# One PSUM tile per bank, an exp per bank, a new recording order and filler products in a scheduled attention-and-convolution kernel

## Chip, cores, metric

The kernel runs on one core of one Trainium2 chip. The metric is device time in microseconds (us) of that core. A run over 1.5% above the fastest of its kernel is counted as slow. The medians below are of all runs, the ratios and their intervals of fast runs alone. The engines are called by their names in the profile: PE (TensorE matmuls), PEld (its weight loads), DVE (VectorE), ACT (ScalarE), POOL (GpSimd) and SP (SyncE, which only starts transfers here).

## The reference

Four batches, eight heads, 768 positions, 64 columns per head. Attention with 8 global keys and a window of 96, whose result `x` (4 x 768 x 512) goes into a gated long convolution. All inputs and outputs are float32.

```python
scores = (q @ k.T) / sqrt(64) + bias                  # bias: -slope[h] * distance
scores = where(is_global | is_local, scores, -1e9)
a = exp(scores - max);  a = a / (a.sum() + 1e-9)
x = (a @ v).transpose(0, 2, 1, 3).reshape(4, 768, 512)
x1, x2, x3 = split(x @ w_proj)                        # 512 columns each
conv = irfft(rfft(x2, axis=1) * rfft(filter), n=768)  # circular convolution over positions
out = (x1 * conv * x3) @ w_out
```

## The kernel before

The kernel first notes down every piece of work as an `Op`: with the engine or engines that may do it, an assumed cost, its inputs and outputs, and the PSUM bank that it fills (`acq`) or reads (`use`). A list scheduler (`Plan.schedule`) then decides engine, bank and order by these costs, and `emit` records the real instructions in the order of the scheduled starts. Waits between engines are not written by hand. The tile layer puts them in from what each recorded instruction reads and writes, by declared tile.

PSUM is declared as four tiles of two banks each. A `Bank` of the plan is one half of such a tile, or a whole one for the scores of two heads:

```python
self.psum = [self.ps.tile([P, 1024], F32, name=f"bank{i}") for i in range(4)]
...
def emit(self, order):
    for o in order:
        a = o.acq
        if a:
            lo = 512 * (a.at % 2)
            a.tile = self.psum[a.at // 2][:, lo:lo + 512 * a.n]
        o.fn(o.eng)
```

The choice of a bank prefers one whose sibling in the same tile is in use, so that pairs stay whole for the scores:

```python
if o.acq.n == 1:
    i = min(range(8), key=lambda i: (max(banks[i], at), banks[i ^ 1] == math.inf
                                      and -1 or 0, -banks[i]))
else:
    i = min((0, 2, 4, 6), key=lambda i: max(banks[i], banks[i + 1]))
```

Scores of a pair of heads fill two banks, and one exp of 864 columns reads both:

```python
def scores(self, hp, gi):
    b = g.bank(2)
    ...                                  # run: products of both heads, one bank per head
    g.op("P", 0.3, run, acq=b, ...)
    g.op("A", act(864), lambda _: nc.scalar.activation(eo, b.f32()..., Act.Exp,
         scale=self.scale), use=[b], w=[("E", hp, gi)], table="exp", name="exp")
    g.op("V", dve(864, 2) + ..., masked, ...)    # times the mask
```

Per batch, PE does: transposes of q and k, scores, values, transposes of the result, the gate's products (x1 and x3), the projection for x2, forward transform, inverse transform, output projection. Between any two of these, ACT or DVE empties banks into SBUF. While one batch is in its convolution, the next is in its attention.

The softmax here doesn't subtract the row's maximum and nothing guards it: scores larger than these inputs give would overflow.

## Time and profile before

| | before |
|---|---|
| time, median of 3 runs given with the kernel | 233.29 us (232.41 to 234.41) |
| time, median of 4 runs, with the profiled one | 232.85 us |
| span in the profile | 232.7 us |
| mean granted clock of PE | 0.947 of full speed |

From the page of the profile, busy time by engine, and then two rows of the span in 40 slices of 5.8 us: PE's busy share in tenths, and PE's granted clock in tenths.

```profile
PE 190.6 (82%) x1630; PEld 111.4 (48%) x1630; DVE 157.6 (68%) x381; ACT 145.1 (62%) x252; POOL 75.0 (32%) x96
...
PE   5473889798996797899989998999979889991871
...
PEclk9997667999999599999999999999999999999799
```

PE is the busiest engine by far, but its row is full of 7s and 8s even in the middle: it stalls often and briefly. The clock row has dips (5, 6, 7), where the throttle granted half speed for a while. The Trainium skill, "TensorE: Matmul & The Clock Gate", Part 1, says that the clock halves after an idle window of about 3.4 us. The trace agrees in the length: its slow stretches last 3.41 or 6.83 us. Before PE's last product there are four: at 20.4 (6.8 us), 30.7 (6.8), 75.0 (6.8) and 215.0 us (3.4). The trace has no record of the clock before 17.0 us, and the row shows 9s there.

The windows view by stage. The borders are the first gate products of batches 0, 1, 2 and 3, the last gate product and the end. Columns: stretch, its length, busy us and count of PE, PEld, DVE, ACT and POOL, granted clock, the transfer engines' share of busy time summed as that view does it, GB/s. (The borders were set 0.2 us ahead of the gate products: the timeline has the first at 36.30 us.)

```profile
36.10:94.30 58.20, 48.60 (x467) 29.90 (x466) 43.05 (x100) 36.20 (x66) 41.06 (x47) 0.93 1.98 121
94.30:129.40 35.10, 32.84 (x274) 18.45 (x275) 23.63 (x61) 22.36 (x40) 5.55 (x7) 1.00 0.60 77
129.40:173.30 43.90, 40.48 (x372) 23.87 (x372) 32.21 (x78) 31.90 (x58) 0.00 (x0) 1.00 0.10 37
173.30:195.60 22.30, 20.17 (x178) 12.03 (x178) 19.70 (x42) 11.47 (x22) 0.00 (x0) 1.00 0.02 8
195.60:232.70 37.10, 24.75 (x110) 10.80 (x107) 11.08 (x21) 16.15 (x32) 0.00 (x0) 0.95 0.21 82
```

PE bounds every stretch, with a few us missing in each; 36 to 94 us is the worst of the middle stages (48.60 of 58.20 us), and in the tail nothing else is left to fill PE (24.75 of 37.10).

From the starts of PE's instructions I split its time into streaming at full clock (what the columns need: 0.216 us per 512), what was lost to a halved clock, and stall. Before: 160.2 + 11.2 + 57.0 us, and the rest is the time before PE's first product. Stall between 40 and 200 us: 32.4 us. The half clock includes the start, where the clock is not recorded. Pages and traces do not give these sums; they are mine.

Where PE's stalls come from is half hidden: they look like ordinary waits for ACT and DVE, and ACT in turn waits for PE. The waits of ACT, by what it was to write and whom it waited for (us in total, times, longest):

```profile
ACT x L310 <- PE bank L682: 14.4, 17, 2.7
ACT eo L306 <- PE bank L746: 10.5, 11, 5.7
...
ACT ot L310 <- PE bank L769: 6.8, 8, 1.1
```

To tell proper waits from others, I matched each wait in the *built* program with its operands: does the wait ask for the instruction that wrote (or last read) this bank, or for a later one? I call the second kind late. Here is one, in the last output projection: the ACT evacuation of the first half of a tile needs PE's instruction no. 3219, but its wait asks for no. 3227, four products later (weight loads are numbered too), into the *other half* of that tile. In the trace that product ended 0.863 us later. The timeline of the tail shows what this looks like. First PE (start, duration, what, in brackets the idle time before and its releaser), then ACT:

```profile
215.02 5.39 PE L746 MATMUL bank<-inv,X 128*128 128x384 f16 x22 [3.65 <-DVE X L806]
221.41 0.59 PE L769 MATMUL bank<-wo,y 128*128 128x512 f16 x2 [1.00 <-ACT eo L306]
222.94 4.92 PE L769 MATMUL bank<-wo,y 128*128 128x512 f16 x22 [0.94 <-DVE y L758]
```

```profile
224.78 1.08 ACT L310 ACTIVATE ot<-bank 128x512 f32<-128x512 f32 x2 [3.42 <-issue]
226.23 1.09 ACT L310 ACTIVATE ot<-bank 128x512 f32<-128x512 f32 x2 [0.36 <-ACT ot L310]
227.95 1.09 ACT L310 ACTIVATE ot<-bank 128x512 f32<-128x512 f32 x2 [0.64 <-ACT ot L310]
```

The output stage begins at 221.41, but the first bank is emptied 3.4 us later, and from then on always two at a time (x2): both halves of a tile come free together.

Last, two groups from the page that the change touches: the exps (shape, count, busy us, mean ns, idle before), and the inverse transform, of which part runs at half clock.

```profile
L588 ACT ACTIVATE E<-bank 128x864 f16<-128x864 f32 x48 | 40.1, 903 | 1.6 <-PE bank L578 1.4
...
L746 PE MATMUL bank<-inv,X 128*128 128x384 f16 x96 | 20.9, 364 | 5.4 <-DVE X L806 3.7
```

### The profile page before, as it was taken

How to read it: one execution, taken by the hardware profiler on the slowest of the kernel's cores; microseconds unless marked ns; L12 is line 12 of the kernel's file. 1: busy time of each engine (PE TensorE's matmuls, PEld its weight loads, DVE VectorE, ACT ScalarE, POOL GpSimd, SP SyncE). 2: the span in 40 equal slices, each digit the busy share in tenths (PEclk: the TensorE clock that was granted, in tenths of full speed). 3: DMA queues.
4: the chain of work that ended last, by engine and by line, in shares of the span. 5: the costliest groups of instructions: out<-in, count | busy, mean ns of one | idle time of the engine just before them, and what ended most of it. 6: DMA issues, size and time to landing. Idle time of an engine off the chain costs nothing. (4 is left out here: it accounts for less than half of the span.)

```text
span 232.7 us, 4288 instructions
## 1 busy us (share of the span) xinstructions
PE 190.6 (82%) x1630; PEld 111.4 (48%) x1630; DVE 157.6 (68%) x381; ACT 145.1 (62%) x252; POOL 75.0 (32%) x96
## 2 busy tenths in 40 slices
PE   5473889798996797899989998999979889991871
PEld 2271656554444565555445656436545545340430
DVE  6894886764789777792188998617888796037230
ACT  4589882436897862524896848569974644662532
POOL 8999638987828636910000000000000000000000
PEclk9997667999999599999999999999999999999799
DMA  7999999999999979992400000150000001500015
GB/s 134 195 156 169 202 191 155 152 145 165 147 110 69 119 51 109 119 114 74 180 3 0 3 1 3 45 202 27 0 0 3 0 3 55 216 0 0 0 46 230
DMA packets 90933, 20.90 MB, mean 90 GB/s; under 512 B 83776, under 2 KB 87840, under 8 KB 90912
## 3 DMA queue, kind: packets, MB, share of 16 engines
q0 software_dynamic: 80912, 12.52, 78.3%
q1 hardware_dynamic: 10000, 8.10, 11.2%
q8 instruction: 13, 0.21, 0.4%
q14 instruction: 8, 0.07, 0.1%
HBM read 26.61 MB, written 6.29 MB: 141 GB/s over the span
## 5 line engine op out<-in xcount | busy, mean ns | idle before, releaser
L682 PE MATMUL bank<-xT,w 128*128 128x384 f16 x256 | 44.3, 329 | 2.6 <-ACT xT L306 1.4
L588 ACT ACTIVATE E<-bank 128x864 f16<-128x864 f32 x48 | 40.1, 903 | 1.6 <-PE bank L578 1.4
L682 PEld LDWEIGHTS <-w 128*128 128x128 f16 x256 | 25.1, 99 | 19.9 <-issue 3.6
L310 ACT ACTIVATE x<-bank 128x384 f16<-128x384 f32 x31 | 15.2, 491 | 25.0 <-PE bank L682 14.4
L600 DVE TENSOR_TENSOR E<-E,mask 128x864 f16<-128x864 f16 x32 | 18.4, 602 | 17.8 <-ACT E L588 17.7
L690 DVE TENSOR_TENSOR g<-bank,x 128x384 f16<-128x384 f32 x32 | 17.8, 557 | 14.2 <-PE bank L682 5.8
L322 POOL DMA_DIRECT2D kn<-in_k_dram x28 | 25.4, 920 | 5.5 <-DMA g<-in_moe_filter_fft_dram 2.9
L322 POOL DMA_DIRECT2D vn<-in_v_dram x28 | 25.0, 914 | 2.3 <-PE bank L625 1.4
L746 PE MATMUL bank<-inv,X 128*128 128x384 f16 x96 | 20.9, 364 | 5.4 <-DVE X L806 3.7
L769 PE MATMUL bank<-wo,y 128*128 128x512 f16 x96 | 22.5, 379 | 2.4 <-ACT eo L306 1.0
L578 PE MATMUL bank<-QT,KT 64*128 64x216 f16 (+2 forms) x224 | 17.1, 263 | 8.0 <-ACT E L588 3.2
L640 DVE TENSOR_TENSOR xn<-bank,rc 128x256 f16<-128x256 f32 (+1 forms) x48 | 22.5, 469 | 1.6
L310 ACT ACTIVATE ot<-bank 128x512 f32<-128x512 f32 x24 | 13.4, 595 | 14.3 <-PE bank L769 6.8
L306 ACT CAST eo<-bank 128x384 f16<-128x384 f32 x29 | 12.8, 488 | 14.0 <-PE bank L746 10.5
L322 POOL DMA_DIRECT2D qn<-in_q_dram x18 | 15.9, 891 | 16.0 <-PE bank L552 8.9
L620 PE MATMUL bank<-vn,E 128*128 128x65 f16 x224 | 18.8, 201 | 2.3 <-DVE xn L640 0.7
L539 PE MATMUL bank<-ab,fwd 128*128 128x512 f16 x72 | 18.3, 379 | 1.3 <-ACT ab L306 0.7
L620 PEld LDWEIGHTS <-E 128*128 128x128 f16 x224 | 16.1, 102 | 6.3 <-DVE E L600 2.9
L625 PE MATMUL bank<-vn,E 128*128 128x65 f16 x192 | 18.5, 200 | 0.0
L306 ACT CAST ab<-bank 128x512 f16<-128x512 f32 x24 | 13.8, 596 | 6.1 <-PE bank L726 4.6
L578 PEld LDWEIGHTS <-KT 64*128 64x128 f16 x224 | 9.3, 99 | 16.3 <-issue 12.8
L746 PEld LDWEIGHTS <-X 128*128 128x128 f16 x96 | 9.8, 109 | 13.2 <-issue 4.9
(100 smaller groups left out, 317.9 us busy)
## 6 DMA issues: line engine op xcount, KB each, us to landing
out_dram<-ot SPq DMA_DIRECT2D x24, 256.0 KB
kn<-in_k_dram POOLq DMA_DIRECT2D x24, 128.0 KB, 5.9
vn<-in_v_dram POOLq DMA_DIRECT2D x24, 128.0 KB, 6.4
qn<-in_q_dram POOLq DMA_DIRECT2D x18, 128.0 KB, 7.2
ot<-in_q_dram SPq DMA_DIRECT2D x6, 256.0 KB
w<-in_moe_w_proj_dram POOLq DMA_DIRECT2D x4, 256.0 KB, 7.0
g<-in_moe_filter_fft_dram POOLq DMA_DIRECT2D x1, 768.0 KB, 13.3
w<-in_moe_w_proj_dram POOLq DMA_DIRECT2D x1, 512.0 KB, 10.3
```

The lines of the kernel that those rows point to most:

```text
L306: {"A": nc.scalar.copy, "V": nc.vector.tensor_copy, "G": nc.gpsimd.tensor_copy}[e](out, in_)
L310: self.nc.scalar.mul(out, in_, c)
L322: return self.g.op(eng, {"G": 0.93, "S": 0.5}[eng], lambda _: e.dma_start(dst, src), w=w, r=r, nbytes=nbytes, name=name, bias=-2000.0 + se ...
L578: nc.tensor.matmul(sp[:, hh, off:off + w], self.KT[hs, hp, P * m:P * m + P], self.QT[hs, hp, KL * m:KL * m + w], start=(off == 0), stop=Tr ...
L588: g.op("A", act(864), lambda _: nc.scalar.activation(eo, b.f32().rearrange("p (h c) -> p h c", h=2)[:, :, 0:432].rearrange("p h (m w) -> p ...
L600: nc.vector.tensor_mul(eo, eo, mk[:, :, 0:2] if gi == 0 else mk[:, :, 1:3])
L620: nc.tensor.matmul(o[:, hh, i], ef[:, at:at + P], vt[:, t, 2 * hp + hh, :], start=first, stop=(t == 0), skip_group_check=True)
L625: nc.tensor.matmul(o[:, hh, i], ef[:, at:at + P], vt[:, t - 1, 2 * hp + hh, :], start=False, stop=True, skip_group_check=True)
L640: nc.vector.tensor_mul(xn[:, ts[0]:ts[0] + nt].rearrange("p t h d -> p h t d"), o[:, :, :, 0:D], r.to_broadcast([P, 2, nt, D]))
L682: nc.tensor.matmul(bk.f32()[:, 0:h], self.w[:, c, o + P * j:o + P * j + P], self.xT[:, c, h * s:h * s + h], start=(c == 0), stop=(c == 3))
L746: nc.tensor.matmul(bk.f32()[:, 0:h], X[:, s, cs], self.inv[:, s, :], start=(s == slots[0]), stop=(s == slots[-1]))
L769: nc.tensor.matmul(bk.f32(), y[:, c, P * t:P * t + P], self.wo[:, c, :], start=(c == 0), stop=(c == 3))
```

## The change

Its parts are: (1) eight tiles of one bank; (2) scores into two separate banks and an exp of 432 columns on each; (3) instructions recorded so that a consumer comes as soon as its producers are recorded, not by scheduled start; (4) products of zeros (`busy`) wherever the scheduler foresees that PE idles; (5), not in the change's own title, new cost figures in the scheduler, a free choice of bank, and the 768-column angle group of the tables split in two so that each fits a bank. The core of the diff:

```diff
-LAT = {"P": 0.22, "A": 0.16, "V": 0.14, "G": 0.12, "S": 0.1}
+LAT = {"P": 0.2, "A": 0.15, "V": 0.12, "G": 0.15, "S": 0.1}
+BEGIN = 1.0
@@ schedule: choice of banks, cost of transfers @@
-                    if o.acq.n == 1:
-                        i = min(range(8), key=... banks[i ^ 1] == math.inf and -1 or 0 ...)
-                    else:
-                        i = min((0, 2, 4, 6), key=lambda i: max(banks[i], banks[i + 1]))
+                    where = sorted(range(8), key=lambda i: banks[i])[:len(o.acq)]
-                dma[0] = max(dma[0], o.start + 1.7) + o.bytes / 300e3
+                dma[0] = max(dma[0], o.end + 1.8) + n * size / (306e3 if size < 512 else 390e3)
-        return out
+        return self.program(self.fill(out))
@@ new @@
+    BUSY = 0.225
+    def fill(self, out):
+        ...
+                gap = o.start - at                      # PE idle in the plan
+                n = int((gap - 0.1) / self.BUSY)
+                if n > 0:
+                    spare = [...]                       # a bank that nobody holds meanwhile
+                    if spare: ...                       # n products of `idle` (zeros) into it
+    def program(out):
+        ...                                             # need[o]: producers, and who held its bank
+        while len(order) < len(out):
+            for e in "AVSGP":                           # PE last
+                if line[e] and need[line[e][-1]] <= done:
+                    o = line[e].pop(); done.add(o); order.append(o)
+                    break
@@ buffers, scores, emit @@
-        self.psum = [self.ps.tile([P, 1024], F32, name=f"bank{i}") for i in range(4)]
+        self.psum = [self.ps.tile([P, 512], F32, name=f"bank{i}") for i in range(8)]
+    def busy(self, n, b):
+        for _ in range(n):
+            self.nc.tensor.matmul(b.f32(), self.idle[:, 0:P], self.idle, start=True, stop=True)
-        b = g.bank(2)
+        bs = [g.bank(), g.bank()]
-        g.op("A", act(864), lambda _: nc.scalar.activation(eo, b.f32()..., Act.Exp, ...), use=[b], ...)
+        for hh in range(2):
+            g.op("A", act(432), lambda _, hh=hh: nc.scalar.activation(
+                eo[:, hh], bs[hh].f32()[:, 0:432]..., Act.Exp, ...), use=[bs[hh]],
+                w=[("E", hp, gi, hh)], ...)
-                a.tile = self.psum[a.at // 2][:, lo:lo + 512 * a.n]
+                b.tile = self.psum[b.at]
```

Left out: the same edit of `acq=b` to `acq=[b]` everywhere, and further cost figures (scores 0.30 to 0.34, values 0.03 per product, transposes of the result 0.06, bank release +0.1).

## The prediction

> **What bounds the kernel now.** The page: PE busy 190.6 of 232.7 us (82%), DVE 68%, ACT 62%. From 36 to 205 us PE is the busiest engine in nearly every 10 us stretch (windows view). Before that data and ACT set the pace: ACT runs without a break from 15.3 to 25.7 us (timeline: masks, first exps), PE only 18.6 us of the first 30. After 205 us nothing overlaps; PE idles about 11 us. Comparing PE's starts in the trace with what the columns need at full clock, I estimate 160 us streaming, 12 us lost to a halved clock (granted clock 0.5 at 20-27, 31-37, 75-82, 215-218 us), 56 us of stalls, 33 of them between 30 and 205 us.
>
> **What the change removes.** I matched the waits of both built programs with their operands. Before, 125 of 169 waits of ACT for PE ask for a later product than the one that wrote the bank being read; so do 36 of 72 of DVE for PE and 94 of 283 of PE for ACT or DVE. After: 0, 0 and 2. In the trace the late part costs ACT about 30 us and PE directly 12.7 us, nearly all where PE is the bound. Zero products: 58; 15 in the start, 13 in the middle, 20 ahead of the last inverse (where PE waits 4.0 us for DVE), 10 ahead of the last output. A 512-column product takes 0.216 us at full clock, so the middle ones cost at most 2.8 us and the 20 fill that gap. The Trainium skill, "TensorE: Matmul & The Clock Gate", Part 1, says an idle window of 3.4 us halves the clock; the trace agrees (slow stretches are 3.41 or 6.83 us long).
>
> **What it adds.** 48 exps of 864 columns become 96 of 432. Back to back, five of 864 took 3.98 us (0.80 each), three of 384 took 1.27 (0.42); estimate 0.46 each, 5 us more ACT in all, 1.5 at the start where ACT is critical.
>
> **On the critical path.** Start to 36 us: up to 1 us lost, 1 to 2 gained by clock. Middle: of 12.7 direct about 10, about 4 from consumers that come sooner, about 4 from the stall at 73-77 us and the half clock after it, less 3 for zero products and exps. Tail: inverse at full clock 1.7 us (22 products at 0.32 now, 0.164 after), evacuations no longer held back in pairs 2 to 3: 4.5. Sum about 20.
>
> **Predicted: 213 us**, 206 to 221 in 8 of 10; faster by over 2% 0.94, within 2% 0.05, slower 0.01.
>
> **What would show it.** ACT idle before x, ot and eo with PE as releaser falls from 32 us to under 12. PE stall between 40 and 200 us roughly halves. Granted clock is 1.0 from 75 us on. The stretch from the last gate product to the end (36.7 us) shrinks to about 32. Up to 36 us nothing moves by over 2 us.
>
> **What would make it wrong.** DVE becomes the limit in the middle, so removed waits return as waits for DVE; loads of the second batch (DMA share over 90% to 85 us) come too late for a faster PE; zero products delay PE where the gap does not exist; the order from new cost figures is worse.

## More of the kernel before

Count of late waits in the built program before:

```
engine that waits <- engine waited for     late / all
ACT <- PE                                    78 / 169
DVE <- PE                                    36 /  72
PE  <- ACT or DVE                            94 / 283
```

For ACT the prediction has 125. That count took the 47 waits of exps for late as well, but one exp of 864 columns reads both halves of its tile, so it needs the later product. A second count, from the kernels built again, gives 78; it confirms the row of DVE, and for PE gives 92 of 281.

## The result, and the profile after

| | before | after |
|---|---|---|
| median of 4 runs | 232.85 us | 207.76 us (206.38 to 208.45) |
| ratio | | 0.8904, 95% interval 0.884 to 0.8969 |
| span in the profile, granted clock | 232.7 us, 0.947 | 204.3 us, 0.982 |

Ratios here are the mean time of one kernel's fast runs over that of the other's fast runs of the same rounds, so not quite the ratio of the medians beside them. The predicted 213 us was 5 us too high; the range held the result.

The page of the kernel after: busy times, PE's row, PE's clock row, and the chain that ended last by engine.

```profile
PE 191.8 (94%) x1688; PEld 111.9 (55%) x1688; DVE 152.2 (75%) x382; ACT 149.4 (73%) x303; POOL 75.5 (37%) x96
...
PE   7993799999998899999999999999999999999992
...
PEclk9998599999999999999999999999999999999999
...
PE 82%; ACT 11%; DVE 4%; issue 2%; ACTq 0%
```

PE's row is 9 almost throughout. Note that busy PE alone does not prove useful work, as 58 of the products are zeros; the sum below takes them out. The chain now runs along PE for 82% of the span. (Before, the chain could be followed for only 3% of the span, so there is nothing to compare.) The windows by the same stages:

```profile
33.00:76.90 43.90, 41.93 (x428) 26.41 (x425) 38.61 (x94) 34.24 (x73) 37.64 (x44) 1.00 2.53 157
76.90:111.00 34.10, 34.06 (x320) 20.05 (x320) 26.07 (x69) 24.89 (x51) 9.97 (x12) 1.00 1.10 106
111.00:151.20 40.20, 40.20 (x391) 24.16 (x388) 32.88 (x80) 32.56 (x71) 0.00 (x0) 1.00 0.13 42
151.20:171.40 20.20, 20.20 (x185) 12.41 (x184) 18.96 (x41) 12.65 (x29) 0.00 (x0) 1.00 0.04 15
171.40:204.30 32.90, 28.82 (x140) 13.36 (x138) 11.06 (x21) 17.39 (x31) 0.00 (x0) 0.99 0.23 88
```

From 76.9 to 171.4 us PE is busy 94.46 of 94.5 us: the records leave no idle time of PE there, so little is left to gain except by less work. The start (up to the first gate) went from 36.1 to 33.0 us, the middle from 159.5 to 138.4, the tail from 37.1 to 32.9. The first stretch of the middle alone gave 14.3 of the 28.4 us. (The profiled run of after is its fastest, 206.38 us; by the medians the gain is 25.1.) The loads that it runs under, which I had feared would be late, came at 157 instead of 121 GB/s.

The sum over PE, in us:

```
                streaming   half clock   stall   zero products   stall 40-200 us
before            160.2        11.2       57.0        0             32.4
after             160.2         6.6       22.6       12.5           12.0
```

The timeline of the tail after, first PE, then ACT:

```profile
185.63 3.19 PE L356 MATMUL bank<-idle 128*128 128x512 f16 x14
188.66 4.32 PE L803 MATMUL bank<-inv,X 128*128 128x384 f16 x24
192.81 2.32 PE L356 MATMUL bank<-idle 128*128 128x512 f16 x10
194.97 5.34 PE L826 MATMUL bank<-wo,y 128*128 128x512 f16 x24
```

```profile
196.09 0.60 ACT L364 ACTIVATE ot<-bank 128x512 f32<-128x512 f32 x1 [2.54 <-PE bank L826]
196.95 0.60 ACT L364 ACTIVATE ot<-bank 128x512 f32<-128x512 f32 x1 [0.27 <-PE bank L826]
```

The first output bank is emptied 1.1 us after its first product started (3.4 before), and then one by one, every 0.86 us, right behind PE's four products. In the built program no wait of ACT or DVE for PE is late any more (0 of 263, 0 of 125), and 2 of 417 of PE for them. The groups of the page and the waits of ACT that answer to those before:

```profile
L645 ACT ACTIVATE E<-bank 128x432 f16<-128x432 f32 x96 | 42.8, 565 | 0.9 <-PE bank L633 0.7
...
L803 PE MATMUL bank<-inv,X 128*128 128x384 f16 x96 | 18.9, 326 | 0.1
L356 PE MATMUL bank<-idle 128*128 128x512 f16 x58 | 17.5, 436 | 1.2 <-DVE warm L424 1.2
```

```profile
ACT x L364 <- PE bank L739: 14.5, 20, 0.9
ACT ot L364 <- PE bank L826: 10.8, 24, 2.5
ACT eo L360 <- PE bank L803: 10.6, 13, 4.5
```

The exps cost ACT 2.7 us more in all (42.8 against 40.1), and the inverse transform no longer stalls PE (0.1 against 5.4 us before it). The waits of ACT hold a surprise: I had predicted that these three would fall from 32 to under 12 us. They went from 31.7 to 35.9 (14.5 + 10.8 + 10.6), though each single wait became shorter (the longest before an x went from 2.7 to 0.9 us). This is explained below.

### The profile page after: what moved, and what is told of

It reads as the page before. It is cut to its first block, busy times and chain, and to the rows that moved or that the text cites. A ratio compares the mean times of both kernels' runs of the same rounds, so it can differ in the third digit from the quotient of the medians.

```text
span 204.3 us, 4516 instructions
## 1 busy us (share of the span) xinstructions
PE 191.8 (94%) x1688; PEld 111.9 (55%) x1688; DVE 152.2 (75%) x382; ACT 149.4 (73%) x303; POOL 75.5 (37%) x96
## 3 DMA queue, kind: packets, MB, share of 16 engines
q1 hardware_dynamic: 10000, 8.10, 12.7%
## 4 chain that ended last, share of the span: by engine, by line
PE 82%; ACT 11%; DVE 4%; issue 2%; ACTq 0%
PE bank L739 20%; PE bank L826 10%; PE bank L783 9%; PE bank L803 8%; PE bank L356 7%; PE bank L595 6%; PE bank L608 5%; ACT E L645 5%; PE bank L633 4%; PE bank L677 4%; PE bank L712 3%; PE bank L682 3%; ACT h L364 2%; ACT mask L551 1%; DVE E L653 1%
## 5 line engine op out<-in xcount | busy, mean ns | idle before, releaser
L739 PE MATMUL bank<-xT,w 128*128 128x384 f16 x256 | 43.9, 326 | 0.0
L645 ACT ACTIVATE E<-bank 128x432 f16<-128x432 f32 x96 | 42.8, 565 | 0.9 <-PE bank L633 0.7
L364 ACT ACTIVATE x<-bank 128x384 f16<-128x384 f32 x31 | 15.7, 506 | 16.3 <-PE bank L739 14.5
L376 POOL DMA_DIRECT2D vn<-in_v_dram x28 | 25.1, 921 | 5.6 <-PE bank L682 4.8
L364 ACT ACTIVATE ot<-bank 128x512 f32<-128x512 f32 x24 | 14.3, 597 | 10.8 <-PE bank L826 10.8
L360 ACT CAST eo<-bank 128x384 f16<-128x384 f32 x29 | 13.7, 490 | 10.7 <-PE bank L803 10.6
L677 PE MATMUL bank<-vn,E 128*128 128x65 f16 x224 | 18.7, 197 | 0.4
L803 PE MATMUL bank<-inv,X 128*128 128x384 f16 x96 | 18.9, 326 | 0.1
L356 PE MATMUL bank<-idle 128*128 128x512 f16 x58 | 17.5, 436 | 1.2 <-DVE warm L424 1.2
L677 PEld LDWEIGHTS <-E 128*128 128x128 f16 x224 | 15.4, 99 | 5.6 <-DVE E L656 1.3
L633 PE MATMUL bank<-QT,KT 64*128 64x216 f16 (+2 forms) x224 | 15.8, 248 | 0.9 <-DVE inv L360 0.2
L608 PE MATMUL bank<-ident,kn 128*128 128x128 f16 x112 | 11.1, 235 | 5.3 <-ACT E L645 4.2
L852 DVE TENSOR_TENSOR p<-X,h 128x1024 f16<-128x1024 f16 x12 | 8.2, 686 | 10.3 <-ACT X L360 10.2
```

The costliest lines, as they stand in the source:

```text
L356: self.nc.tensor.matmul(b.f32(), self.idle[:, 0:P], self.idle, start=True, stop=True)
L364: self.nc.scalar.mul(out, in_, c)
L376: return self.g.op(eng, 0.57 + 0.00035 * nbytes[0] if eng == "G" else 0.5, lambda _: e.dma_start(dst, src), w=w, r=r, nbytes=nbytes, name= ...
L633: nc.tensor.matmul(bs[hh].f32()[:, off:off + w], self.KT[hs, hp, P * m:P * m + P], self.QT[hs, hp, KL * m:KL * m + w], start=(off == 0), s ...
L645: g.op("A", act(432), lambda _, hh=hh: nc.scalar.activation(eo[:, hh], bs[hh].f32()[:, 0:432].rearrange("p (m w) -> p m w", m=2), Act.Exp, ...
L677: nc.tensor.matmul(o[:, hh, i], ef[:, at:at + P], vt[:, t, 2 * hp + hh, :], start=first, stop=(t == 0), skip_group_check=True)
```

## The experiments

The theory after the result: the gain comes from the tiles. With two banks in one declared tile, a wait for one bank becomes a wait for whatever touched the other, so PE, ACT and DVE hold each other up. Rivals: the gain comes from the recording order, from the zero products (clock), or from the new cost figures. Ratios are to the kernel before, run beside each kernel on the same chip.

One comparison needs no chip. I built the kernel after with the old recording order. On PE, ACT, DVE and SP the built program is the same instruction for instruction, waits included; only register names in 14 POOL instructions differ (seven that set a register, seven that use it). The same holds for e3 and e9 below. With eight tiles the new recording order does nothing. The runs below show what it does with four.

**e1: after, with banks in pairs again.** Plan, order and zero products are those of after; only the declaration differs.

```diff
-        self.psum = [self.ps.tile([P, 512], F32, name=f"bank{i}") for i in range(8)]
+        self.psum = [self.ps.tile([P, 1024], F32, name=f"bank{i}") for i in range(4)]
-                b.tile = self.psum[b.at]
+                b.tile = self.psum[b.at // 2][:, 512 * (b.at % 2):512 * (b.at % 2) + 512]
```

> The changed kernel, instruction for instruction in the same order on every engine, but its eight banks declared as four tiles of two, so that only the waits differ. Counted in the built program: 244 of 296 waits of PE for ACT or DVE ask for a later instruction than the one that used the bank (after: 2 of 417), 5 of 383 waits of ACT or DVE for PE (after: 0). Theory 'precise waits': most of the gain goes, 222 to 234 us, and PE stalls return between 40 and 190 us with ACT and DVE as releasers. Rival 'clock' (the zero products hold the clock up, and that is the gain) and rival 'order' (the new cost figures made a better order): both are kept here, so 206 to 211 us.

Measured: 316.51 us, ratio 1.3639 (1.3518 to 1.3759). PE's sum: 160.2 streaming, 29.6 half clock, 109.6 stall, of which 100.1 us ended with a late wait. Page rows of PE and its clock, then the groups of PE's gate products and scores, with idle before and its releasers:

```profile
PE   5473777887795665767784688889786787899994
...
PEclk9996555999599857695999597999967999999999
```

```profile
L739 PE MATMUL bank<-xT,w 128*128 128x384 f16 x256 | 50.2, 347 | 6.8 <-ACT x L364 2.4 <-ACT KT L360 1.8 <-DVE g L747 1.4
L633 PE MATMUL bank<-QT,KT 64*128 64x216 f16 (+2 forms) x224 | 23.4, 276 | 20.2 <-ACT E L645 14.3 <-DVE KT L360 1.0 <-DVE xn L697 0.9
```

The same gate products in the kernel after, in that view:

```profile
L739 PE MATMUL bank<-xT,w 128*128 128x384 f16 x256 | 43.9, 326 | 0.0
```

The scores now wait 14.3 us for an exp that they do not need, and the clock falls again and again. Matching waits with operands shows how: 244 of PE's 296 waits for ACT and DVE are late, while only 5 of the 383 in the other direction are. Since each consumer is recorded right behind its producer, PE's next product into the neighbour bank finds that consumer ahead of it on the same tile and has to wait for it. So the tiles matter, in the direction of the theory, and by far more than I had allowed for.

**e2: e1 with the old recording order** (`return self.fill(out)` in place of `self.program(self.fill(out))`).

> As e1_pairs, and the recording order also as before (by scheduled start, not consumers right behind their producers). Order on each engine the same again. In the built program 201 of 333 waits of PE for ACT or DVE are late, and 118 of 298 of ACT or DVE for PE. With eight tiles the built program is the same with and without the new recording order, so this part can only act with paired tiles. Theory 'precise waits': 222 to 236 us, within 5 us of e1_pairs, as lateness only moves from PE to ACT and DVE. If the recording order matters by itself, e2 is over 8 us slower than e1. Rivals 'clock' and 'order of the schedule': 206 to 211 us.

Measured: 240.87 us, ratio 1.0326 (1.0264 to 1.0387). Now 118 of 298 waits for PE and 201 of 333 of PE are late; stall 51.4 us. My idea that the order merely moves the lateness from one side to the other was wrong: with pairs, the order is worth 76 us between e1 and e2. Recording by scheduled start is much the better order when banks are coupled, and it makes no difference when they are not.

**e3: after without its 58 zero products** (`return self.program(out)`).

> The changed kernel without its 58 zero products; all else in the same order, two waits late. Theory 'precise waits': 207 to 213 us; the last inverse runs at half clock again (1.7 us lost), the start has the cold clock to about 17 us, and the 17 small products (3.7 us at most) come back as gain. Rival 'clock': 222 us or more, granted clock under 0.95.

Measured: 207.35 us (206.79 for its three fast runs), ratio 0.8874 (0.8805 to 0.8942), the same as after. The zero products keep the clock up in the tail, as intended; the clock row and PE's tail without them:

```profile
PEclk9999599999999699999999999999999999996698
```

```profile
188.31 6.46 PE L803 MATMUL bank<-inv,X 128*128 128x384 f16 x22 [4.42 <-DVE X L863]
...
196.92 4.92 PE L826 MATMUL bank<-wo,y 128*128 128x512 f16 x22 [1.73 <-DVE y L815]
```

The last inverse takes 6.46 us instead of 4.32, behind 4.42 us of idle PE; with 20 zero products in that gap it runs at full clock. So what the fillers win in the tail they must lose elsewhere. (The 40 to 200 us stall is 18.7 us here and 12.0 in after, but there the zero products themselves take room.)

**e4: before, with the new recording order alone.** `program` is adapted to banks of two; the plan is that of before.

```diff
-        return out
+        return self.program(out)
```

> The kernel before with the new recording order alone (each engine's order as before). In the built program late waits of ACT and DVE for PE fall from 161 of 241 to 49 of 336, those of PE for ACT and DVE rise from 94 of 283 to 171 of 261. Theory 'precise waits': a trade of one for the other, 228 to 238 us, no gain over 2%. Rival 'consumers behind producers is what removes the waits': under 222 us.

Measured: 348.29 us (344.49 and 346.15 in its two fast runs), ratio 1.482 (1.47 to 1.4941). I had expected one lateness traded for the other without a loss; the trade is there, and it is dear. Stall is 147.3 us, of which 124.5 ended with a late wait. PE's largest waits (us, times, longest):

```profile
PE bank L709 <- ACT x L337: 8.6, 14, 0.6
PE bank L709 <- DVE g L717: 7.1, 9, 1.2
```

Gate products wait for the evacuation of gate products in the other half of their tile. (The 161 and 49 late waits in the expectation count exps of both halves as late; without them it is 114 before and none here. So this order does clear every late wait for PE, and pays for it with PE's own.) Of the four parts in the change's title, this one alone would have made the kernel half as slow again.

**e5: after once more**, beside e6 to e8 on the same chip, for comparison.

> The changed kernel itself, on the chip of the next two runs, to compare with them: 206 to 208.5 us.

Measured: 207.16 us, ratio 0.889 (0.8852 to 0.8928).

**e6: zero products in the tail only** (the groups of 20 and 10).

```diff
-                if n > 0:
+                if n >= 10:
```

> The changed kernel with the two large groups of zero products alone (20 ahead of the last inverse, 10 ahead of the last output), none of the other 28. If the 17 small ones cost PE time where it is saturated (3.7 us at most) and the 11 of the start gain nothing, as data and ACT set the pace there: 203 to 206 us, 2 to 4 us under the changed kernel. If the start's warm clock matters: 207 us or more, and the first gate product comes later.

Measured: 205.26 us (204.28 to 206.12), ratio 0.8804 (0.8767 to 0.8841). The interval does not touch that of e5. This is the best version found, and it beats both kernels. PE's sum: 6.9 half clock, 26.3 stall, 6.5 zero products.

**e7: zero products in groups of 5 and more**: as e6 (`n >= 5`), which adds 11 at the start to the 30 of the tail.

> The changed kernel with groups of at least five zero products alone (5 and 6 in the start, 20 and 10 in the tail). Same as e6 within 1 us if the start does not matter, 1 to 3 us under e6 if the start's warm clock does.

Measured: 208.79 us, ratio 0.8952 (0.8909 to 0.8996). So 11 zero products at the start cost 3.5 us. The first evacuation of the angle tables in e6, then the same in e7, and what PE does ahead of it in e7:

```profile
3.51 0.60 ACT L460 ACTIVATE y<-bank 128x512 f32<-128x512 f32 x1 [1.27 <-PE bank L496]
```

```profile
4.56 0.60 ACT L460 ACTIVATE y<-bank 128x512 f32<-128x512 f32 x1 [2.33 <-PE bank L496]
```

```profile
1.19 2.31 PE L356 MATMUL bank<-idle 128*128 128x512 f16 x5 [1.19 <-DVE warm L424]
3.44 0.60 PE L490 MATMUL bank<-row 1*128 1x512 f16 x1
```

The plan saw a gap in PE before the angles; on the chip five zero products at a cold clock took 2.31 us, and the angles stood behind them. The masks on ACT then began at 15.71 instead of 14.27 us, and the first gate at 32.85 instead of 31.26. Of the 3.5 us in the medians the profiles show 1.6 (205.0 against 203.4 us in span); the profiled run was e7's fastest (207.12 us), and the rest I cannot place. Nor is it shown that the late gate is the path of the cost. In e3, whose work before the tail is that of e6, the first gate came at 32.52 us, and in e11 below at 33.60, yet their second batch's gates began at 76.47 and 76.77 us, about as in e6 (76.43; e7: 78.15).

**e8: eight tiles with the old cost figures, no zero products. A mistake.** I meant to restore the old figures (latencies, costs, transfer model), but gave rows of 256 bytes half their old rate:

```diff
-                dma[0] = max(dma[0], o.end + 1.8) + n * size / (306e3 if size < 512 else 390e3)
+                dma[0] = max(dma[0], o.start + 1.7) + n * size * (2 if size == 256 else 1) / 300e3
```

> Eight tiles and an exp per bank, no zero products, and the scheduler's figures (durations, latencies, DMA) as in the kernel before. Theory 'precise waits': 205 to 213 us, within 3% of e3_nofill. Rival 'new figures made a better order, and that is a large part of the gain': 216 us or more.

Measured: 220.16 us, ratio 0.9449 (0.9394 to 0.9503). At first this looked as if the new figures were worth half the gain. Then I saw that the scheduler had planned the first batch's gates at 53.8 us instead of about 32: it believed that the loads would be late. In the trace they do begin at 54.07 us. The run stays as a by-product: that one wrong figure in the model costs 10 us against e9.

**e9: e8 mended**: all old figures as they were (the line above without the factor of two), eight tiles, an exp per bank, no zero products.

> e8_oldfig_nofill mended: there the DMA figure was set by mistake to half the kernel before's rate, so it did not test the old figures (its gates of the first batch began at 53.8 us instead of 32 us). Here all figures are the kernel before's. Eight tiles, an exp per bank, no zero products. Theory 'precise waits': 205 to 212 us, within 2.5% of e3_nofill (207.4). Rival 'new figures gave half the gain', as e8 seemed to say: 216 us or more.

Measured: 210.11 us, ratio 0.901 (0.8962 to 0.9057). The new figures are thus worth about 3 us (e3: 207.35, or 206.79 in its fast runs), not half. Late waits: none for PE, 3 of 420 of PE.

**e10: e9 with pairs**, recorded by scheduled start as before did: e1's edit on e9, and `return out`.

> e9's order on every engine, but four tiles of two banks, recorded by scheduled start: 172 of 333 waits of PE for ACT or DVE late, 124 of 280 of ACT or DVE for PE. Against e9 this is the worth of the eight tiles at the old figures. 'Precise waits': 232 to 245 us, 25 us or more above e9. If the eight tiles were worth only part of the gain: under 225 us.

Measured: 244.87 us, ratio 1.0489 (1.0429 to 1.0549). With the same plan, figures and exps, and the recording order that suits the pairs, the declaration alone is worth 34.8 us. (e9 was recorded by `program`, but its built program is the same without it, as said above.) 124 of 280 waits for PE and 172 of 333 of PE are late, stall is 65.5 us (e9: 35.0), half clock 14.0 (e9: 8.7). Some 37 us of e10's stall of PE ended with a late wait, and some 1 us of e9's, by matching trace and built program once more. One group of PE, values, with idle before it and its releasers, in e9 and then in e10:

```profile
L677 PE MATMUL bank<-vn,E 128*128 128x65 f16 x224 | 18.4, 197 | 0.7 <-DVE E L653 0.3 <-DVE E L656 0.2
L677 PE MATMUL bank<-vn,E 128*128 128x65 f16 x224 | 19.6, 203 | 6.1 <-ACT E L645 1.6 <-ACT QT L360 0.9 <-DVE xT L360 0.8
```

In e10 the values wait for copies of the transposed q (QT), which they do not read.

**e11: e6 with the transposes of the inverse tables held until the masks are made**, to see if ACT, which paces the start, would begin its masks earlier.

```diff
-                                                        for c in range(2)])
+                                                        for c in range(2)],
+                 after=[x for x in g.ops if x.name == "mask"])
```

> A version to beat both: e6_tailfill, with the 18 transposes of the inverse table and their evacuations held until the masks are made, so that ACT comes to the masks and exps of the first batch about 1.5 us sooner. If ACT sets the pace of the start: masks from about 12.5 us (e6: 14.0), first gate 1 to 2 us sooner, 203 to 205 us. If data does: the same as e6, 204 to 206.5 us.

Measured: 205.55 us, ratio 0.8814 (0.8775 to 0.8854): no difference from e6. ACT's timeline shows why:

```profile
12.38 0.58 ACT L360 COPY QT<-bank 128x512 f16<-128x512 f16 x1 [1.86 <-PE bank L609]
12.98 1.28 ACT L552 ACT_TABLE_LOAD   x1
14.27 5.17 ACT L552 ACTIVATE mask<-dm 128x648 f16<-128x648 f32 x8
```

The two copies of the tables (1.52 us in e6) are gone from before the masks, but ACT idles for PE's transposes of q instead, and the masks begin at 14.27 us as in e6. What sets that time lies further up, and was not tested. The first gate came later than in e6 (33.60 against 31.26 us) without a change of the total.

**e12: before with two exps of 432 columns per pair**, inside one `Op`, so that plan and pairs stay.

```diff
-        g.op("A", act(864), lambda _: nc.scalar.activation(eo, b.f32()..., Act.Exp, ...), use=[b], ...)
+        def exps(_):
+            for hh in range(2):
+                nc.scalar.activation(eo[:, hh], b.f32()[:, 512 * hh:512 * hh + 432]..., Act.Exp, ...)
+        g.op("A", act(864), exps, use=[b], w=[("E", hp, gi)], table="exp", name="exp")
```

> The kernel before with its 48 exps of two banks as 96 of one bank each, in the same tiles and the same places. Busy ACT from 145 to 148-150 us. As ACT is critical only at the start, 233 to 238 us; more than that, over 240 us, if the paired tiles make more of the extra instructions.

Measured: 234.32 us, ratio 1.0021 (0.9955 to 1.0086). ACT is busy 2.5 us more in all (147.6 against 145.1), and the time does not move. The Trainium skill, "Perfetto Trace Analysis", Optimizing Scalar/DVE Operations, says that breaking up instructions may help where they cause bubbles on other engines. Here the split alone neither helps nor harms, since both exps still read one tile. It is needed for the tiles of one bank, and its price is small. The Trainium skill, "ScalarE: Activation LUTs", What ACT_TABLE_LOAD costs, gives the time of an instruction with immediate scale and bias, as these are: 186 ns plus 0.833 ns per column, with about 93 ns of overlap back to back. By estimate from that page it is 906 ns for 864 columns and 546 for 432; the profile shows means of 903 and 564. Each split should then add 93 ns, 4.5 us for 48; the exps of e12 took 2.7 us more (42.8 against 40.1), so here the estimate is too high.

The steps together, each with its median (ratios to before, taken in several groups of runs; e1 to e12 ran on three chips):

```
before                                                     ~232.7   1
+ two exps per pair                             (e12)      234.32   1.002
+ free choice of bank, angle group split        (e10)      244.87   1.049
+ eight tiles, recorded by program()            (e9)       210.11   0.901
+ new cost figures                              (e3)       207.35   0.887
+ 58 zero products                              (after)    207.76   0.890   (e5: 207.16, 0.889)
only the 30 zero products of the tail           (e6)       205.26   0.880
```

## Why the prediction was right, and where it was off

**The bound and the cause: right.** The prediction said that PE bounds the kernel and that late waits, which the eight tiles take away, are the main loss. e9 against e10 shows it with all else held: 34.8 us. The built programs (94 of 283 late waits of PE before, 2 of 417 after) and PE's stall (57.0 to 22.6 us) say the same.

**Why 34.8 us by tiles, when the whole change brings 25.** Before had a cure of its own: its choice of bank, which prefers the sibling of a bank in use, and its order. e10 has pairs without that choice and is 12 us slower than before; e12 shows that the exps are not the reason. So some 10 us of the pairs' price had been hidden by tuning around it. e10 differs from e12 in the bank choice (the scores of a pair may now lie in two tiles, with an `Op` for each exp) and also in the split of one angle group, and these were not separated.

**The middle: mechanism right, size too small, by two other terms.** The prediction's term was "Middle: of 12.7 direct about 10, about 4 from consumers that come sooner, about 4 from the stall at 73-77 us and the half clock after it, less 3", together 15 us. Measured: 21.1 (159.5 to 138.4). The stall between 40 and 200 us fell by 20.4 us (32.4 to 12.0), to 37%, where I had said "roughly halves" (a second count by a like sum gave 30.0 to 13.7, or 46%). By the trace of before, only 15.8 us of PE's whole stall ended with a late wait. That consumers which are not held up free their banks and feed the next stage sooner is argued, not measured. What was mis-sized can be read from e9 and e3, both without zero products, though from one profile each. From before to e9 (old figures) the middle fell by 17.4 us (159.5 to 142.1), where the terms without the "less 3" make 18. With the new figures it took 138.2 us (e3), 3.9 us less, a gain that the prediction had at nothing; and in after, with the zero products, 138.5, so the 3 us to be lost were not lost. (These traces are from several chips.) 14.3 us came in the first stretch (58.2 to 43.9), where the loads kept up and the half-clock stretch at 75.0 us is gone.

**The tail: right.** Said 4.5 us, measured 4.2. Both parts are in the timelines: the inverse from 5.39 us (22 products) to 4.32 (24), where 1.7 us was said, and the output stage from its first product to the end from 11.3 to 9.3 us. They make 3.1 of the 4.2; the rest lies ahead of them.

**The start: small, but over the limit that I set.** "Up to 36 us nothing moves by over 2 us": the first gate moved by 3.1 us (36.1 to 33.0).

**The marker that failed.** "ACT idle before x, ot and eo with PE as releaser falls from 32 us to under 12": it rose to 35.9. The step behind it was that this idle time was the cost of late waits. It was not: ACT is not the bound, and it must idle for as long as PE sets the pace (before 62% busy, after 73%). What the late waits changed was the length and number of its waits: before an x, 17 waits of up to 2.7 us became 20 of up to 0.9. The idle time that should have been marked was PE's own.

**Zero products and clock: half right.** Predicted and seen: granted clock 1.0 in the middle and at the last inverse. I had counted about 4 us for the stall at 73-77 us and the half clock behind it to the middle, and 1.7 for the tail's clock, as gains of the change. But e3, with no zero products, is as fast as after. The tail's 30 seem to gain 1.6 to 2 us (e3 to e6, though these two intervals overlap), and the other 28 cost 1.9 (e6 to e5, whose intervals do not). The up to 2.8 us that I had put down to the middle ones are not there: from the second batch's first gate to the last gate product, with 8 of the zero products in it, after and e5 took 94.5 us, e3 and e6 94.3. Most of the cost is there by the second batch's first gate, which came at 77.73 us in e5 and 76.43 in e6. e7 points to the 11 larger ones at the start, but they cost more alone (3.5 us) than the 28 together, with intervals of e5 and e7 that overlap; the path of this cost stays open. The clock row of e6 has two dips, at 17 and 69 us, and e5 has dips at about the same places in spite of its fillers, so the fillers there do not even keep the clock up reliably.

**Cost figures: named only as a risk, "the order from new cost figures is worse".** They were a gain of about 3 us (e9 to e3; the intervals do not overlap, but the runs are from two chips). Which of the figures does it was not tested. The mistake in e8 shows how strong such a figure can be.

**Exps: too dear.** Estimated 5 us more of ACT; measured 2.7, and no time (e12).

So 213 us missed 207.76 by the middle, where the new cost figures and a loss that did not come seem to make up the 6 us, and by little else.

## What to carry to other kernels

Declare one tile per PSUM bank when the framework tracks waits by tile, and check it in the built program: match each wait with the operand that it is for, and count those that ask for a later instruction than they need. A plan, a bank choice or an order that has been tuned around coupled buffers can hide a part of their price and make any other change look bad (recording consumers early: 348 us with pairs, no change at all without). Put fillers only where the trace shows a long gap on a path that ends the kernel, judge progress by the idle time of the bounding engine rather than by that of an engine that waits for it, and test each part of a bundle alone: here one of four did nearly all.

## What the Trainium skill lacked or had wrong

- No page says that waits can be tracked by declared PSUM tile, so that a tile of two banks couples both. "PSUM — Partial Sum Buffer", PSUM bank collisions raise a hardware error, has the rule to guard PSUM by bank and quadrant, by bank being the simple version. The runs agree that by bank is enough here: all of them, with PE filling banks while ACT and DVE emptied others, gave correct results. Missing is the warning that a guard by pairs of banks costs much: 244.87 us against 210.11 at the same plan (e10, e9), and 316.51 against about 207 in the recording order of after (e1, e5).
- "Perfetto Trace Analysis", Optimizing Tensor Performance, Matmuls, counsels that independent groups of products rotate through different banks so that evacuation overlaps. Both kernels rotate; what defeated it before was the declaration. The same page's Optimization Strategy takes consistent bubbles as a sign that buffers may have run out; here there were eight banks in both kernels, and only their declaration differed between e10 and e9 (PE's stall 65.5 and 35.0 us).
- "TensorE: Matmul & The Clock Gate", Part 1, does not say whether products of zeros count as activity for the clock gate. They do: with 20 of them ahead of the last inverse it took 4.32 us, without them 6.46 (after, e3).
- The same Part 1 does not say that warming products have a price: 11 of them at the start, foreseen as free by the plan, made the kernel 3.5 us slower (e7 against e6).
- The rule of that Part cited above, an idle window of about 3.4 us, alone does not explain the trace: of the four slow stretches of before only that at 215.0 us follows such a window. Ahead of the others PE was busy for 1.8 to 2.5 of 3.41 us.
- No page warns that idle time of a non-bounding engine may rise in a better kernel: ACT's idle before three outputs went from 31.7 to 35.9 us while the kernel became 11% faster.
